# Eight small slope diagonals in the opening of an attention kernel: six built by ScalarE ahead of its first cast, two by VectorE behind its own

## The chip, the cores and the metric

The kernel runs on one core of one Trainium2 chip. The metric is the device time in microseconds (us) of one execution. A profile covers one execution; its "span" is about 2 us shorter than the device time of the same run. Engines are named as in the profile: PE (TensorE matmul), PEld (its weight load), DVE (VectorE), ACT (ScalarE), POOL (GpSimd), SP (SyncE).

## The reference, cut to what matters

```python
# attention: 4 batches, 8 heads, 768 positions, head size 64; local window of 96 plus 8 global keys
scores = q @ k.T / 8
bias = -slopes[:, None, None] * dist        # one slope per head
a = softmax(where(keep, scores + bias, -1e9))
x = a @ v
# then a two-layer block over 3072 tokens of 512 (2048 hidden): relu(x @ w_in) squared, scaled and shifted, @ w_out
```

For the first two granules (256 query positions each) the kernel adds the bias by matmul: a diagonal matrix with the head's slope on it, times a common distance matrix, summed in PSUM (the tiles `ps_s` in the profile, which the matmuls write) under the scores. These eight 128x128 diagonals are what the change moves.

## The kernel before

The emission order is each engine's instruction order (ScalarE's timeline below shows its diagonals, cast, diagonals and copy in this order). These are the opening's parts; cuts are marked.

```python
    # POOL: loads of later blocks (each keeps GpSimd busy for 0.8 to 1.0 us in this trace)
    load_qk(1, 0)
    load_v(0)
    load_qk(1, 1)
    load_w_in(0, 8)
    ...
    def diagonal(hs):
        for h in hs:
            nc.scalar.activation(diag[:, h, :], ident_bf[:], ACT.Copy, scale=slopes[h] / QSCALE)

    diagonal(range(0, 4))
    ...
    cp = nc.vector.tensor_copy
    acp = nc.scalar.copy
    ...
    warm(9, 4 * P)            # nine 128x512 matmuls on zeros
    cast_first(0, 0, cp)      # VectorE: first keys, f32 to bf16
    cast_first(0, 1, acp)     # ScalarE: first queries
    diagonal(range(4, H))     # ScalarE: heads 4 to 7
    qk_first(0, 0, cp)        # TensorE transposes keys; VectorE copies them out of PSUM
    qk_first(0, 1, acp)       # TensorE transposes queries; ScalarE copies them out
    open_bias((0, 1))         # TensorE: diagonals of heads 0 to 3 times the distances
    cast_first(1, 0, cp)
    cast_first(1, 1, acp)
    for part in range(2):
        for i in (0, 1):
            u[i][1](part)     # TensorE: first score matmuls
    run(u[0][2])
    warm(4)
    ...
    open_scores((2,))
    make_koff(1, [0])
    qk_block(1, 0, (cp, cp))
    open_bias((3,))
    open_scores((3,))
    stage_A(0)                # first use of the value loads
    ...
    stage_A(2)
    qk_block(1, 1, (cp, acp)) # transposes of key and query block 1: last load of the opening
```

The softmax here doesn't subtract the row's maximum and nothing guards it: scores larger than these inputs give would overflow.

Of the kernel before, what the change touches and what calls it, by code (L numbers as in the profile page):

```python
# [17 lines left out]
def kernel(  # L18
# [13 lines left out]
    nc = tc.nc  # L32
    P = nc.NUM_PARTITIONS

    B, H, S, D = q.shape
# [17 lines left out]
    QSCALE = 1.0 / float(D) ** 0.5  # L53
# [130 lines left out]
    ident_bf = const.tile([P, P], BF16, name="ident_bf")  # L184
# [42 lines left out]
    slopes = [float(2.0 ** (-8.0 * (h + 1) / H)) for h in range(H)]  # L227
    diag = open_bf[:, 3 : 3 + H, :]

    def diagonal(hs):  # L230
        for h in hs:
            nc.scalar.activation(diag[:, h, :], ident_bf[:], ACT.Copy, scale=slopes[h] / QSCALE)  # L232

    diagonal(range(0, 4))

    tmpl = const.tile([P, H, 6, P], BF16, name="tmpl")

# [20 lines left out]
    def cast_first(h2, n, copy):  # L258
        hs = slice(h2 * H // 2, (h2 + 1) * H // 2)
        copy(  # L260
            nat[0][:, n, :, hs, :],
            first_f32[h2, n][:].rearrange("p h (s d) -> p s h d", s=GB),
        )
# [57 lines left out]
    def qk_first(h2, n, evac):  # L321

        ps = ps_h.tile([P, GB, 2, P], BF16, name="ps_t", tag="psh")
        for i in range(GB):
            for c in range(2):
                hp = 2 * h2 + c
                nc.tensor.transpose(
                    ps[:, i, c, :], nat[0][:, n, i, 2 * hp : 2 * hp + 2, :], ident_bf[:]
                )
        dst = qk_of(0, n)[:, 0:GB, 2 * h2 : 2 * h2 + 2, :]  # L330
        evac(  # L331
            dst.rearrange("p b c (m s) -> p c b m s", s=GB),
            ps[:].rearrange("p s c (b m) -> p c b m s", b=GB),
        )
# [675 lines left out]
    warm(9, 4 * P)  # L1010
    cast_first(0, 0, cp)
    cast_first(0, 1, acp)
    diagonal(range(4, H))
    qk_first(0, 0, cp)
    qk_first(0, 1, acp)
    open_bias((0, 1))
# [234 lines left out]
```

## Time and profile before

The time is 208.95 us (median of three runs, 208.86 to 208.96). The profiled run has a span of 206.6 us; at 208.37 us it was faster than any of the three.

| reading | value | view |
|---|---|---|
| TensorE busy | 201.7 of 206.6 us | page, part 1 |
| TensorE's share of the chain that ended last | 95% | page, part 4 |
| four diagonals between cast and copy | 0.90 us on ScalarE | timeline |
| last query transpose ends | 5.92 + 0.22 = 6.14 us | timeline, single matmul |
| query copy starts | 6.24 us | timeline |
| first score matmuls | 6.86 us | chain |

The page of before: engine, busy us, share, instruction count; then shares of the chain of waits by engine.

```profile
PE 201.7 (98%) x2191; PEld 160.2 (78%) x2191; DVE 159.7 (77%) x336; ACT 128.6 (62%) x200; POOL 70.1 (34%) x90
...
PE 95%; DMA 2%; ACT 1%; DVE 0%; issue 0%
```

The chain of waits of before, cut to the first 10 us. Columns: start, us, what.

```profile
0.74 4.14 DMA first<-in_q_dram
...
4.91 0.62 ACT nat L260
5.53 0.81 ACT open_bf L232 x4
6.33 0.48 ACT qx L331
...
6.86 0.51 PE ps_s L441 x12
```

The chain puts 0.81 us on the four diagonals (`open_bf` L232) because they are the last thing ahead of the copy in ScalarE's order. What they cost is only how much longer they last than the copy's other condition, the query transposes. The timeline of ScalarE of before (columns: start, us, engine, line, operation, out<-in, count, idle time before and what ended it):

```profile
3.17 0.91 ACT L232 ACTIVATE open_bf<-ident_bf 128x128 bf16<-128x128 bf16 x4
4.91 0.62 ACT L260 CAST nat<-first 128x512 bf16<-128x512 f32 x1 [0.83 <-DMA first<-in_q_dram]
5.43 0.90 ACT L232 ACTIVATE open_bf<-ident_bf 128x128 bf16<-128x128 bf16 x4
6.24 0.56 ACT L331 COPY qx<-ps_t 128x512 bf16<-128x512 bf16 x1
6.89 0.62 ACT L260 CAST nat<-first 128x512 bf16<-128x512 f32 x1
```

ScalarE idles for 0.83 us ahead of the cast, room for more diagonals. And the eight first transposes of before (durations in ns: minimum, median, maximum):

```profile
L327 PE MATMUL ps_t<-ident_bf,nat x8: 219/288/314, 5.3 to 5.9; 128*128 128x128 bf16 x8
```

VectorE of before, where three operations took longer than their size asks (later in the same trace a 128x512 cast takes 0.44 us, and a 128x128 bf16 copy 0.20):

```profile
2.72 0.64 DVE L192 CAST open_bf<-rel 128x256 bf16<-128x256 f32 x1
...
3.62 0.50 DVE L194 TENSOR_SCALAR open_bf<-open_bf 8x128 bf16<-8x128 bf16 x1
...
4.44 0.79 DVE L260 CAST nat<-first 128x512 bf16<-128x512 f32 x1 [0.32 <-DMA first<-in_k_dram]
```

### The profile page before, as it was taken

How to read it: one execution, taken by the hardware profiler on the slowest of the kernel's cores; microseconds unless marked ns; L12 is line 12 of the kernel's file. 1: busy time of each engine (PE TensorE's matmuls, PEld its weight loads, DVE VectorE, ACT ScalarE, POOL GpSimd, SP SyncE). 2: the span in 40 equal slices, each digit the busy share in tenths (PEclk: the TensorE clock that was granted, in tenths of full speed). 3: DMA queues.
4: the chain of work that ended last, by engine and by line, in shares of the span. 5: the costliest groups of instructions: out<-in, count | busy, mean ns of one | idle time of the engine just before them, and what ended most of it. 6: DMA issues, size and time to landing. Idle time of an engine off the chain costs nothing.

```text
span 206.6 us, 5323 instructions
## 1 busy us (share of the span) xinstructions
PE 201.7 (98%) x2191; PEld 160.2 (78%) x2191; DVE 159.7 (77%) x336; ACT 128.6 (62%) x200; POOL 70.1 (34%) x90
## 2 busy tenths in 40 slices
PE   7999999999999999999999999999999999999993
PEld 2678884557867585878888898888888889888883
DVE  7586589977989866799799975699866696737974
ACT  4975669486976558685664595663695764476200
POOL 8995333899357300913700908200000000000000
PEclk9999999999999999999999999999999999999999
DMA  6999999999999999999999999993460300240006
GB/s 166 172 179 201 207 207 177 155 153 134 126 146 118 155 140 209 206 193 212 139 217 160 118 155 195 189 189 57 53 206 3 98 9 0 61 145 0 0 9 197
DMA packets 110836, 28.17 MB, mean 136 GB/s; under 512 B 97852, under 2 KB 109308, under 8 KB 110812
## 3 DMA queue, kind: packets, MB, share of 16 engines
q0 software_dynamic: 76000, 13.11, 87.6%
q1 hardware_dynamic: 33612, 14.13, 39.5%
q10 hardware_dynamic: 1200, 0.59, 1.1%
q8 instruction: 17, 0.28, 0.6%
q14 instruction: 7, 0.06, 0.1%
HBM read 27.26 MB, written 6.29 MB: 162 GB/s over the span
## 4 chain that ended last, share of the span: by engine, by line
PE 95%; DMA 2%; ACT 1%; DVE 0%; issue 0%
PE ps L619 41%; PE ps L819 24%; PE ps L667 14%; PE ps_s L441 6%; PE ps_av L495 5%; DMA first<-in_q_dram 2%; PE ps_t L351 1%; PE ps_s L517 1%; PE ps_x L591 1%; PE ps_s L532 1%; PE ps_av L558 1%; ACT qx L331 1%; PE ps_t L341 0%; PE ps_last L819 0%; ACT open_bf L232 0%; ACT nat L260 0%
## 5 line engine op out<-in xcount | busy, mean ns | idle before, releaser
L619 PE MATMUL ps<-xT,w_in_bf 128*128 128x256 bf16 x768 | 90.3, 273 | 0.0
L629 ACT ACTIVATE gT<-ps 128x512 bf16<-128x512 f32 x96 | 55.8, 598 | 46.8 <-PE ps L619 46.6
L619 PEld LDWEIGHTS <-w_in_bf 128*128 128x128 bf16 x768 | 73.0, 98 | 9.4 <-DVE xT L594 0.2
L450 ACT ACTIVATE pt<-ps_s 128x1024 bf16<-128x1024 f32 (+1 forms) x44 | 39.3, 946 | 2.7 <-PE ps_s L441 2.7
L667 PE MATMUL ps<-w_out_bf,gT 128*128 128x512 bf16 x128 | 29.7, 380 | 0.0
L457 DVE TENSOR_TENSOR pt<-pt,tmpl 128x1024 bf16<-128x1024 bf16 (+1 forms) x40 | 24.5, 645 | 3.8 <-ACT pt L450 3.7
L819 PEld LDWEIGHTS <-gsum 128*128 128x128 bf16 x256 | 24.1, 98 | 3.7 <-DVE gsum L782 0.5
L108 POOL DMA_DIRECT2D vb<-in_v_dram x24 | 21.6, 915 | 6.3 <-DMA w_out_bf<-in_moe_w_out_dram 3.3
L793 DVE TENSOR_TENSOR gT<-gT 128x1024 bf16<-128x1024 bf16 x20 | 13.7, 686 | 11.7 <-ACT gT L629 11.7
L667 PEld LDWEIGHTS <-gT 128*128 128x128 bf16 x128 | 11.8, 98 | 13.0
L466 DVE TENSOR_TENSOR xn<-ps_av,rc 128x256 bf16<-128x256 f32 x48 | 20.4, 424 | 1.7
L819 PEld LDWEIGHTS <-gT 128*128 128x128 bf16 x200 | 18.6, 98 | 2.3
L465 DVE RECIPROCAL rc<-ps_av 128x4 f32<-128x4 f32 x48 | 8.6, 179 | 12.3 <-PE ps_av L495 10.4
L495 PEld LDWEIGHTS <-pt 128*128 128x128 bf16 x320 | 14.4, 98 | 2.7 <-DVE xn L466 0.7
L116 POOL DMA_DIRECT2D nat<-in_k_dram x16 | 14.4, 897 | 5.5 <-DMA w_in_bf<-in_moe_w_in_dram 2.4
L116 POOL DMA_DIRECT2D nat<-in_q_dram x16 | 14.2, 888 | 4.9 <-DMA nat<-in_q_dram 3.1
L632 DVE TENSOR_TENSOR gT<-gT 128x512 bf16<-128x512 bf16 x32 | 12.9, 421 | 3.6 <-ACT gT L629 3.3
L495 PE MATMUL ps_av<-vb,pt 128*128 128x65 bf16 x208 | 15.4, 193 | 0.0
L819 PE MATMUL ps<-w_out_bf,gsum 128*128 128x256 bf16 x128 | 15.3, 273 | 0.0
L819 PE MATMUL ps<-wsub,gsum 128*128 128x256 bf16 x128 | 15.1, 273 | 0.0
L122 POOL COPY gate<-xT 1x1 bf16<-1x1 bf16 x6 | 1.9, 313 | 36.7 <-DMA xT<-xn 36.7
L819 PE MATMUL ps<-w_out_bf,gT 128*128 128x256 bf16 x120 | 13.9, 273 | 0.0
(111 smaller groups left out, 226.6 us busy)
## 6 DMA issues: line engine op xcount, KB each, us to landing
out_dram<-o_q SPq DMA_DIRECT2D x15, 256.0 KB, 2.4
vb<-in_v_dram POOLq DMA_DIRECT2D x24, 128.0 KB, 7.4
nat<-in_k_dram POOLq DMA_DIRECT2D x22, 128.0 KB, 7.0
nat<-in_q_dram POOLq DMA_DIRECT2D x22, 128.0 KB, 6.7
w_out_bf<-in_moe_w_out_dram POOLq DMA_DIRECT2D x4, 512.0 KB, 16.1
w_in_bf<-in_moe_w_in_dram POOLq DMA_DIRECT2D x4, 256.0 KB, 7.4
w_in_bf<-in_moe_w_in_dram POOLq DMA_DIRECT2D x2, 512.0 KB, 11.2
out_dram<-o_sb SPq DMA_DIRECT2D x4, 256.0 KB, 6.3
```

What stands on the lines that cost most here:

```text
L108: nc.gpsimd.dma_start(vbuf[b % 2][:, sb, :, 0:D], rows_of(v, b, sb))
L116: nc.gpsimd.dma_start(t[:, n, i, :, :], rows_of(srcs[n], b, sb))
L450: nc.scalar.activation(pt[:, :, 0:ncol], ps[:, :, 0:ncol], ACT.Exp, scale=QSCALE)
L457: nc.vector.tensor_tensor(pv, pv, m.rearrange("p h a c -> p h (a c)"), ALU.mult)
L466: nc.vector.tensor_tensor(dst, av[:, :, :, 0:D], rc[:].to_broadcast((P, 2, 2, D)), ALU.mult)
L495: nc.tensor.matmul(av[:, i, hi, 0 : D + 1], lhsT=pt[:, hi, c * P : (c + 1) * P], rhs=vv, start=(n == 0), stop=(n == len(terms) - 1),)
L619: nc.tensor.matmul(ps[:, i, :], lhsT=w_in_bf[:, kc, fc * P : (fc + 1) * P], rhs=xT[j][:, kc, :], start=(kc == 0), stop=(kc == KC - 1),)
L629: nc.scalar.activation(gs, ps[:], ACT.Relu)
L632: nc.vector.tensor_tensor(gs, gs, gs, ALU.mult)
L667: nc.tensor.matmul(po[:], lhsT=g_of(j)[:, fc, tb * P : (tb + 1) * P], rhs=w_out_bf[:, fc, :], start=(fc == 0), stop=(fc == FC - 1),)
L793: outs.append(lambda: nc.vector.tensor_tensor(gs, gs, gs, ALU.mult))
L819: nc.tensor.matmul(ps[:, tb, cs], lhsT=stat[:, fc, tb * P : (tb + 1) * P], rhs=mov[:, fc, cs], start=(fc == 0), stop=(fc == NH - 1),)
```

## The change

Its intent is to leave nothing between ScalarE's cast and its copy of the queries, by using idle time of ScalarE (before the cast) and of VectorE (between its cast and its copy).

```diff
-    diagonal(range(0, 4))
+    diagonal(range(0, 6))
@@
     cast_first(0, 0, cp)
     cast_first(0, 1, acp)
-    diagonal(range(4, H))
+    for h in range(6, H):
+        nc.vector.tensor_scalar_mul(diag[:, h, :], ident_bf[:], slopes[h] / QSCALE)
     qk_first(0, 0, cp)
```

The instruction order of each engine is otherwise the same; TensorE's is the same matmul for matmul, so one can subtract the start of the n-th matmul in one trace from that in another.

## The prediction

> **What bounds the kernel now.** The chain of waits that ended last is 95% TensorE; TensorE is busy 201.7 of 206.6 us at clock 1.0, and by the table of stretches idles only 1.2 us at the start, 0.07 us between 5.28 and 6.90 us, 0.28 us between 8.4 and 10 us, a little at the end. VectorE and ScalarE count only where they hold TensorE up. In the chain, cut to the first 10 us, the lines that the change touches are: load of q (to 4.89), ScalarE cast (4.91), four diagonals (5.53 to 6.33), query copy (6.33 to 6.81), then the first score matmuls (6.86). The intent is to take those four diagonals off that chain.
>
> **Costs.** A diagonal on ScalarE lasts 293 ns and starts 0.20 us after the one before (timeline). [...] Two more ahead of the first cast end near 4.5 us; ScalarE waits for q until 4.91 anyway: free. On VectorE the two multiplies take about 0.18 us each (estimate from the 128x128 bf16 copy, 0.20 us). They start near 5.2 us, behind the key cast, and VectorE idles until the key copy at 5.93: also free, if not held up.
>
> **What is saved.** Not 0.8 us. The query copy needs the query transposes, which TensorE ends at 6.14 (timeline of single matmuls); the copy starts at 6.24 today. So at most about 0.08 us of the four diagonals is exposed. Behind it, TensorE works on bias matmuls until 6.79 and the key copy's weight load comes at 6.72, so the score matmuls can move from 6.86 to about 6.80: 0.06 us. The second q load lands near 6.85 (issue plus 5.6 us), so the second cast, at 6.89, will not move; TensorE does not wait for it, since warm-up matmuls run to 7.91. From there TensorE runs nearly gap-free, so 0.06 us should reach the end.
>
> **What may eat it.** [...] three VectorE ops that began 0.35 to 0.40 us into a load's descriptor writing took 0.64, 0.50 and 0.79 us (the last a cast that took 0.44 us later). The new multiplies begin about 0.28 us into one. If both are blocked the key copy slips by up to 0.1 us; if they block GpSimd, the next query load (lands 11.92, used near 12.06) slips and TensorE may lose up to 0.15 us. I expect one multiply to slip in and the other to wait till about 5.7 us: no harm.
>
> **Prediction.** 208.95 - 0.05 = 208.90 us, between 208.6 and 209.15 (8 in 10). Faster by over 2%: 0.005; within 2%: 0.99; slower by over 2%: 0.005.
>
> **What would show it.** Right: ScalarE has six diagonals from 3.17, none between cast and copy; query copy starts near 6.16; score matmuls near 6.80; second cast still at 6.89; key copy still at 5.93. Wrong: the key copy starts after 6.0 or the score matmuls not before 6.86 (no gain), the transposes at 11.86 show a wait for a load (loss), or a gain over 0.2 us, which would mean that something later hung on this and my reading of the nearly gap-free TensorE was too simple.
>
> **What would make it wrong.** A shift of GpSimd's loads that meets TensorE later, or drift between sessions; both are as large as the gain itself.

Two passages are cut where marked: a formula for ScalarE beside the measured 293 ns, and what was said of GpSimd and VectorE before the three operations. The sum is 208.95 - 0.05 = 208.90 us, the 0.05 standing for the gain that "What is saved" puts at 0.06. "What may eat it" rests on the three operations alone. Its "descriptor writing" is what the trace shows as DMA_DIRECT2D on GpSimd, 0.8 to 1.0 us a load and without a break from 1.34 to 13.1 us; the three operations began 0.37, 0.40 and 0.35 us into one. That they were blocked by it was the author's estimate.

## The result, and the profile after

The changed kernel took 208.70 us (median of four runs, 208.63 to 209.15); the kernel before, with the run added in that session, 208.91 us (208.52 to 208.96). The ratio is 0.9999 with a 95% interval of 0.998 to 1.0017. Ratios here are the mean time of one kernel's runs over the mean of the other's in the same rounds, so not quite the ratio of the medians.

The profiled run happened to be the slowest of the four (209.15 us, span 207.4). Its page:

```profile
PE 202.1 (97%) x2191; PEld 160.1 (77%) x2191; DVE 161.3 (78%) x338; ACT 128.5 (62%) x198; POOL 68.9 (33%) x90
...
PE 65%; DMA 23%; POOL 9%; issue 1%; DVE 0%; POOLq 0%
```

TensorE is as busy as before. Its share of the chain fell because this chain runs back from a late wait at 69 us (below) through loads and GpSimd.

ScalarE after:

```profile
3.17 1.31 ACT L232 ACTIVATE open_bf<-ident_bf 128x128 bf16<-128x128 bf16 x6
4.94 0.62 ACT L260 CAST nat<-first 128x512 bf16<-128x512 f32 x1 [0.46 <-DMA first<-in_q_dram]
6.05 0.58 ACT L331 COPY qx<-ps_t 128x512 bf16<-128x512 bf16 x1 [0.49 <-PE ps_t L327]
6.88 0.62 ACT L260 CAST nat<-first 128x512 bf16<-128x512 f32 x1 [0.25 <-DMA first<-in_q_dram]
```

The copy now waits for the transposes, as intended, and starts 0.20 us sooner. But the transposes end sooner too: 6.01 instead of 6.14. They are faster, each of them, though the change touches none:

```profile
L327 PE MATMUL ps_t<-ident_bf,nat x8: 219/219/230, 5.3 to 5.8; 128*128 128x128 bf16 x8
```

The first score matmuls after (6.86 before):

```profile
6.68 0.51 PE L441 MATMUL ps_s<-qx,kx 64*128 64x128 bf16 x12
```

VectorE after:

```profile
4.49 0.75 DVE L260 CAST nat<-first 128x512 bf16<-128x512 f32 x1 [0.36 <-DMA first<-in_k_dram]
5.16 0.72 DVE L1014 TENSOR_SCALAR open_bf<-ident_bf 128x128 bf16<-128x128 bf16 x2
5.73 0.69 DVE L331 COPY kx<-ps_t 128x512 bf16<-128x512 bf16 x1
```

The two multiplies end at 5.88, one after 0.18 us and the other after 0.63; the key copy starts 0.04 us after the last key transpose, as before.

Now the subtraction, matmul for matmul, after minus before (start times from the trace's records):

| at (us in before) | matmul | after minus before |
|---|---|---|
| 6.86 | first scores | -0.17 |
| 10.53 | third matmul of the first `stage_A`, the first that reads value block 1 | -0.12 |
| 12.11 | fifth transpose of key and query block 1, the first that reads the query load | -0.07 |
| to 59.1 | all | -0.06 |
| 68.4 | third score matmul of a later block | +0.73 |
| end | last matmul | +0.74 |

So 0.17 us were won in the opening, 0.10 given back by 12.1 us, and in this run 0.8 lost at 59 and 68 us. The large one is a wait for a transposing DMA, seen in the timeline of TensorE after:

```profile
68.36 0.23 PE L441 MATMUL ps_s<-qx,kx 64*128 64x128 bf16 x2
69.10 0.34 PE L441 MATMUL ps_s<-qx,kx 64*128 64x128 bf16 x6 [0.51 <-DMA qx<-nat]
```

The other three timed runs of the changed kernel took 208.63 to 208.72 us, so this 0.8 us is no fixed cost. The questions are: why was the opening's gain 0.17 us and not the predicted 0.06, what clips it, and is the late wait the change's doing?

### The profile page after: what moved, and what is told of

The parts are those of the page before. It is cut to its first block, busy times and chain, and to the rows that moved or that the text cites. A ratio compares the mean times of both kernels' runs of the same rounds, so it can differ in the third digit from the quotient of the medians.

```text
span 207.4 us, 5323 instructions
## 1 busy us (share of the span) xinstructions
PE 202.1 (97%) x2191; PEld 160.1 (77%) x2191; DVE 161.3 (78%) x338; ACT 128.5 (62%) x198; POOL 68.9 (33%) x90
## 4 chain that ended last, share of the span: by engine, by line
PE 65%; DMA 23%; POOL 9%; issue 1%; DVE 0%; POOLq 0%
PE ps L619 29%; PE ps L819 24%; DMA nat<-in_q_dram 12%; DMA w_in_bf<-in_moe_w_in_dram 6%; PE ps L667 5%; DMA qx<-nat 4%; PE ps_s L441 4%; PE ps_av L495 3%; POOL vb L108 3%; POOL nat L102 3%; POOL w_in_bf L140 2%; POOL nat L116 1%; PE ps_last L819 0%; DVE o_last L828 0%; POOL rel L173 0%
## 5 line engine op out<-in xcount | busy, mean ns | idle before, releaser
L465 DVE RECIPROCAL rc<-ps_av 128x4 f32<-128x4 f32 x48 | 8.6, 179 | 12.3 <-PE ps_av L495 10.4
L122 POOL COPY gate<-xT 1x1 bf16<-1x1 bf16 x6 | 1.1, 176 | 35.9 <-DMA xT<-xn 35.9
## 6 DMA issues: line engine op xcount, KB each, us to landing
w_in_bf<-in_moe_w_in_dram POOLq DMA_DIRECT2D x2, 512.0 KB, 11.3
```

## The experiments

Two theories of the faster transposes. A: TensorE starts at half speed, and the moment at which it gets full speed differs from run to run, whatever the kernel. B: the change did it, for example by keeping ScalarE off the identity matrix that the transposes read. No run had shown either yet; both rest on one difference between two profiles, transposes 0.107 us apart in before and 0.056 in after.

### The kernel before again, and the changed kernel again

No edit in either.

> The kernel before, unchanged. Theory A (clock phase): the 0.107 us spacing of the first transposes in the profile of before (half speed until 5.79 us) against 0.056 us in that of after is not the change: [...] the first score matmuls start anywhere from 6.68 to 7.3 us. Theory B (the change moved them): the transposes are at half speed until 5.8 us again, score matmuls at 6.86. Time 208.9, spread of single runs 0.4 us, ratio 1.000.

> The changed kernel, unchanged. Theory A: the clock switch moves here too; the query copy starts 0.04 us after the last query transpose whatever the clock does (before: 0.10 us). Theory B: full speed from 5.29 again, score matmuls at 6.68. The stall of 0.5 us at 68 us for the transposed queries, seen once in the profile of after, comes and goes with the loads: single runs from 208.5 to 209.2. Ratio to before 0.9995 to 1.000.

What is cut from the first is a range for the moment of the switch that no run had shown; the measured moments follow.

Measured: before again 208.62 us (208.43 to 208.92), ratio 0.9994 (0.9982 to 1.0006); after again 208.61 (208.39 to 209.63), ratio 0.9997 (0.9981 to 1.0013), both against 208.86 (208.56 to 209.1). The single runs of after again spread wider than the expected 208.5 to 209.2. The unchanged kernel, second profile: the transposes, ScalarE and the first scores:

```profile
L327 PE MATMUL ps_t<-ident_bf,nat x8: 289/314/314, 5.3 to 6.0; 128*128 128x128 bf16 x8
...
5.36 0.90 ACT L232 ACTIVATE open_bf<-ident_bf 128x128 bf16<-128x128 bf16 x4
6.38 0.59 ACT L331 COPY qx<-ps_t 128x512 bf16<-128x512 bf16 x1
...
7.33 0.28 PE L441 MATMUL ps_s<-qx,kx 64*128 64x128 bf16 x4
```

Here all eight transposes ran at half speed: most took 314 ns, 0.107 us apart, where after has 219 ns and 0.056 us (the clock records of before and after hold two values, 1.0 and 0.5), and full speed comes only after them. The times of these clock records are in the packed traces and no `prof` view prints them. They have the switch to full speed at 5.82 us in the first profile of before, 7.04 in before again, 5.14 in after and 4.97 in after again; the warm-up matmuls began at 1.19 in all four. Over the ten runs told here whose first matmul came at 1.19 us with at least nine warm-ups the switch came between 3.95 and 7.04 us, so 2.8 to 5.8 us after that matmul. In all the traces told here, every stretch at full speed lasted a whole number of times 3.413 us (2, 58, 59 or 61; 201.39 us, 59 times, in before and in after). Two runs further on rule out B: the kernel before (loads late) was at full speed from 5.48, the changed kernel (loads late) at half until 6.24. So A stands.

Two things follow. First, the unchanged kernel's first scores came at 7.33 us here against 6.86 in its first profile, +0.47, and its last matmul came 0.48 us later too: a delay of the opening goes to the end undiminished, and the clock's moment alone moves this kernel by more than the whole expected gain. (At half speed the first scores do not even wait for the copy, which ended at 6.96: the bias matmuls of `open_bias` kept TensorE busy until then.) Second, the diagonals ended at 6.26, before the last transpose (6.03 + 0.31 = 6.34). The copy waited for the transposes alone: in this run there was nothing for the change to save.

After again had full speed, 219 ns per transpose, but its first query load came late (cast at 5.15), and the first scores started at 6.89. Measured from the cast's end (5.77) they took 1.13 us, as in the first profile of after.

### Four more diagonals in the way; the VectorE half left out

```diff
 # on the kernel before
     diagonal(range(4, H))
+    diagonal(range(4, H))
```

> Kernel before, its four diagonals between cast and copy done twice (eight in all). ScalarE then ends them near 7.13 us and the query copy starts near 7.05 instead of 6.24. Theory 1 (the opening is on the chain and TensorE is gap-free after it): the first score matmuls come near 7.67 us and the run takes 0.8 us longer, 209.7. Rival (waits for loads further on take up what the opening loses): under 0.3 us longer.

```diff
 # on the changed kernel
-    for h in range(6, H):
-        nc.vector.tensor_scalar_mul(diag[:, h, :], ident_bf[:], slopes[h] / QSCALE)
+    diagonal(range(6, H))
```

> Changed kernel, but the last two diagonals stay on ScalarE between cast and copy, none on VectorE. They should end near 5.95 us, before the query transposes (6.01 to 6.14), so the copy starts as in the changed kernel, 0.04 us after the last transpose: same time. If instead the VectorE half matters, the copy is late by up to 0.1 us, or the VectorE ops after the key cast (the cast at 6.33, the koff copies at 8.7 and 9.3, which the changed kernel's profile shows longer than before's) get back to 0.44, 0.34 and 0.18 us.

Measured: four more diagonals gave 209.64 us (209.43 to 210.26), ratio 1.005 (1.0035 to 1.0064), which on 208.86 is +1.0 us with 0.7 to 1.3 as the interval. Its ScalarE:

```profile
5.05 0.62 ACT L260 CAST nat<-first 128x512 bf16<-128x512 f32 x1 [0.97 <-DMA first<-in_q_dram]
5.58 1.70 ACT L232 ACTIVATE open_bf<-ident_bf 128x128 bf16<-128x128 bf16 x8
7.18 0.56 ACT L331 COPY qx<-ps_t 128x512 bf16<-128x512 bf16 x1
```

The copy started 1.51 us after the cast's end (5.67), where 0.72 + 0.80 was expected. Against before, the first scores came 0.94 us later and the last matmul 1.04. The opening is on the chain and its losses are paid in full; theory 1 stands.

Without the VectorE half: 208.58 us (208.5 to 208.89), ratio 0.9992 (0.9979 to 1.0005).

```profile
5.04 0.62 ACT L260 CAST nat<-first 128x512 bf16<-128x512 f32 x1 [0.56 <-DMA first<-in_q_dram]
5.57 0.50 ACT L232 ACTIVATE open_bf<-ident_bf 128x128 bf16<-128x128 bf16 x2
6.36 0.59 ACT L331 COPY qx<-ps_t 128x512 bf16<-128x512 bf16 x1 [0.28 <-PE ps_t L327]
```

With two diagonals left between cast and copy, ScalarE still idled for 0.28 us before the copy. This run was at half speed up to 6.18 us. At full speed the two would end 0.41 us after the cast (6.07 - 5.66) and the transposes 0.45 us after it (6.01 - 5.56 in after), so even then they should not be in the way; that is an estimate from these two traces. So the VectorE half was needed neither at this run's clock, nor, by the estimate, at full speed. Of the VectorE times that the expectation names, the second key cast was back at 0.44 us, but the two koff copies (`make_koff`) took 0.29 and 0.64; in before again they took 0.77 and 0.60, so they vary without the change.

### Forcing the clock

To compare both kernels at full speed, the first loads were issued late, behind idle activations, with longer warm-up.

```diff
 # on either kernel
+    pause = const.tile([P, 2 * P], F32, name="pause")
+    ... nine activations pause<-pause on ScalarE, then all four first loads issued by ScalarE
-    warm(9, 4 * P)
+    warm(24, 4 * P)
```

> Kernel before with the first loads issued by ScalarE alone after nine idle activations, and 24 warm-up matmuls: TensorE must then be at full speed when the first q comes, and GpSimd's loads land long before they are used. Theory (the four diagonals are exposed by what they last beyond the query transposes, and that depends on the clock): the query copy starts about 0.72 us after the cast's end, 0.26 us after the last query transpose. Total about 212.

> The changed kernel with the same late loads. Theory: the query copy starts 0.04 us after the last query transpose, about 0.22 us sooner after the cast than in the run above; the first score matmuls come about 0.2 us sooner after the cast, and the total is 0.2 us (0.1%) less than above. Rival (the change is worth 0.06 us at most, whatever the clock): both copies within 0.1 us of each other.

Both missed the state that they were made for: 219.17 us (218.01 to 219.5) and 218.03 (217.57 to 218.39), where 212 was expected. Issued from 5.62 us on, the first keys came near 11.6 and 11.3 us, about 6 us after issue (in before they landed 3.7 us after it), the first queries near 13.1 and 12.1; I take it that they stood in line with GpSimd's loads. TensorE idled for 2.79 and 2.65 us before its first transposes. In the first run the query transposes were at half speed and the copy started 0.05 us after them; in the second they were still at full speed and it started 0.04 us after them. (From the cast's end it was 0.72 and 0.49 us, as expected.) The two were not in the same state, and their difference in time is not used.

The opposite, half speed in both:

```diff
 # on either kernel
-    warm(9, 4 * P)
+    warm(2, 4 * P)
```

> Kernel before with two warm-up matmuls in place of nine. Theory (clock): TensorE is at half speed through the whole opening, the query transposes end near 6.35, later than the diagonals, the copy starts 0.04 us after them, and the first score matmuls come at 7.3 or later; the run is 0.5 to 1.5 us longer than before. Rival (the clock plays no part): the copy starts at 6.24 as in the first profile of before and the time is the same.

> The changed kernel with two warm-up matmuls in place of nine. Theory: no diagonal is exposed in either, so query copy and first score matmuls stand as far behind the q cast as in the run above, within 0.05 us, and the times agree within their spread. Rival (the diagonals cost 0.06 us or more whatever the clock): copy and score matmuls come sooner after the cast than above.

Measured: 210.34 us (209.51 to 210.54), ratio 1.0071, and 210.50 (209.91 to 210.57), ratio 1.0088. Full speed now came at 8.55 and 9.37 us by the clock records. Seven warm-up matmuls fewer cost 1.5 to 1.8 us (0.0071 and 0.0088 of 208.64), more than anything the change touches. The intervals of the two ratios overlap (1.005 to 1.0092 and 1.0072 to 1.0103). Before at half speed:

```profile
5.37 0.90 ACT L232 ACTIVATE open_bf<-ident_bf 128x128 bf16<-128x128 bf16 x4
6.37 0.59 ACT L331 COPY qx<-ps_t 128x512 bf16<-128x512 bf16 x1
```

After at half speed:

```profile
6.40 0.58 ACT L331 COPY qx<-ps_t 128x512 bf16<-128x512 bf16 x1 [0.70 <-PE ps_t L327]
```

The copies start 0.04 us after the last query transpose in both (6.34 and 6.36), the first scores at 7.55 and 7.58. The expectation had put them the same distance behind the cast; that was wrong, since the cast ended 0.24 us apart (5.46 and 5.70) and the slow transposes, not the cast, set the time. The point holds: at half speed the change saves nothing.

Then full speed again, with the first query cast alone held back:

```diff
 # on either kernel, behind the diagonals ahead of the cast
+    ...                       # the tile pause, cleared by VectorE
+    for _ in range(13):
+        nc.scalar.activation(pause[:], pause[:], ACT.Copy, scale=1.0)
-    warm(9, 4 * P)
+    warm(26, 4 * P)
```

> Repair of the two warm_late runs, which missed: their loads came so late that TensorE fell back to half speed. Here the loads stay as they are; 13 idle activations hold only the first q cast back to about 9.8 us, and 26 warm-up matmuls bridge the wait, so TensorE is at full speed at the query transposes. Kernel before otherwise. Theory: the query copy starts 0.72 us after the cast's end and about 0.26 us after the last query transpose. Total about 214.2.

> The changed kernel with the same two additions. Theory: the copy starts 0.49 us after the cast's end, 0.04 us after the last query transpose, so 0.22 us sooner than above; the loads land long before they are used, so the 0.2 us reach the end: ratio to the run above 0.999. Rival (the change is worth at most 0.06 us at any clock, or is lost later): copies within 0.1 us, last matmuls within 0.1 us.

Measured: before 213.38 us (213.37 to 213.39, four runs); after 214.29 (213.29 to 214.9, six runs in three clumps: 213.3, 213.8, 214.8). Before, all transposes at full speed:

```profile
10.61 0.40 PE L332 MATMUL ps_t<-ident_bf,nat 128*128 128x128 bf16 x4 [1.52 <-ACT nat L265]
...
10.46 0.90 ACT L232 ACTIVATE open_bf<-ident_bf 128x128 bf16<-128x128 bf16 x4
11.27 0.56 ACT L336 COPY qx<-ps_t 128x512 bf16<-128x512 bf16 x1
```

The last query transpose ended at 11.00 and the copy started 0.26 us after it: as expected. A copy that waits for nothing else starts 0.04 us after it, so 0.22 us of the diagonals is exposed at full speed. The run of after missed its state. Its profile got full speed early, at 3.95 us, so it ended the warm-up early, idled longer, and fell back to half speed:

```profile
8.16 0.39 PE L332 MATMUL ps_t<-ident_bf,nat 128*128 128x128 bf16 x4
10.72 0.59 PE L332 MATMUL ps_t<-ident_bf,nat 128*128 128x128 bf16 x4 [2.17 <-ACT nat L265]
```

Four equal transposes took 0.39 us before an idle time of 2.17 us and 0.59 after it. The clock record has the fall at 10.78, at the end of a stretch of 3.41 us in which TensorE had been busy for 1.24. In before with the cast held back, four transposes still took 0.40 us after 1.52 us without a matmul, in a stretch of 3.41 us with 1.67 us busy. The totals of this pair therefore compare two clock states and not the change. The record lists the mean granted clock of every run: 0.990 in the three runs of after at 214.8 to 214.9, 0.998 to 1.0 in the other three and in all runs of before. So the upper clump is such a state; 213.8 against 213.3 stays unexplained. The two runs of after at 213.3 (213.29 and 213.31) lie 0.06 to 0.10 us below all four of before; picked afterwards as they are, they are a hint of a gain and no more.

### The loads that clip the gain

In the table above the gain shrinks at the first matmul that reads value block 1 and at the first transpose that reads query block 1. The value load was issued by GpSimd at 4.09 and landed 6.3 us later, at about 10.4 (DMA view of after); the matmul before it started at 10.33, it itself at 10.42, 0.09 us apart where before shows 0.04. In after again the same gap was 0.14 us, with that load landing near 10.6. The query load was issued at 5.81 and landed near 12.0; the transpose started at 12.04. Each of the three waiting matmuls began 0.04 to 0.05 us after the landing. My theory was that GpSimd's issuing sets these times.

```diff
 # on either kernel
     load_v(0)
+    late_f = const.tile([P, 2 * P], F32, name="late_f")
+    for _ in range(3):
+        nc.gpsimd.iota(late_f[:], ...)     # idle work, about 1 us
     load_qk(1, 1)
```

> Kernel before with three idle iotas (about 1 us) on GpSimd ahead of the loads of key and query block 1, whose query load landed near 12.0. Theory (that load caps what the opening can gain): the fifth of the block's eight transposes starts near 13.0 whatever the clock and the opening did before; all later work is 0.5 to 0.9 us later than usual, total 209.5. Rival (the load has slack): the total does not change.

> The changed kernel with the same three iotas. Theory: the fifth transpose starts at the same time as in the run above within 0.05 us, although the first score matmuls may start up to 0.5 us apart; so the change is worth nothing here and the totals agree. Rival: the difference at the first score matmuls is still there behind the transposes.

Measured: 208.73 us (208.53 to 208.86), ratio 1.0002 (0.9985 to 1.0018), and 208.78 (208.36 to 209.1), ratio 1.0001 (0.9984 to 1.0018). The rival of the first run won: no change. The rival of the second won too: the first scores of the two runs stood 0.13 us apart (6.88 and 7.01), and so did the fifth transposes (12.14 and 12.27), which both came after the landing and did not wait. GpSimd in before:

```profile
4.95 0.90 POOL L102 DMA_DIRECT2D nat<-in_k_dram  x1
5.82 0.91 POOL L102 DMA_DIRECT2D nat<-in_q_dram  x1
```

GpSimd with the iotas, on the kernel before:

```profile
4.97 1.34 POOL L201 IOTA late_f<- 128x256 f32 x3
6.26 1.05 POOL L102 DMA_DIRECT2D nat<-in_k_dram  x1
7.30 0.88 POOL L102 DMA_DIRECT2D nat<-in_q_dram  x1
```

The query load was issued 1.48 us later (7.30 against 5.82) and the DMA view has it landing after 4.6 us instead of 6.1: at 11.94 and 11.96. In that stretch the DMA view (6 to 12 us, both runs) shows the engines busy for 90% or more of every slice, so I take it that they set the landing and that GpSimd only lengthens or shortens the line. So the clip is real (the waits of 0.05 to 0.1 us in the two profiles of after), but when GpSimd issues the query load is not its cause. The value load was issued ahead of the iotas, so its landing was not tested, and no run here moved either.

One of these runs gave by luck what the forced pairs had missed. The kernel before with iotas got full speed at 5.48 us and its query cast at 4.93, within 0.01 us of the first profile of after:

```profile
L333 PE MATMUL ps_t<-ident_bf,nat x8: 219/220/286, 5.3 to 5.8; 128*128 128x128 bf16 x8
...
4.93 0.62 ACT L266 CAST nat<-first 128x512 bf16<-128x512 f32 x1 [0.85 <-DMA first<-in_q_dram]
5.45 0.90 ACT L238 ACTIVATE open_bf<-ident_bf 128x128 bf16<-128x128 bf16 x4
6.26 0.56 ACT L337 COPY qx<-ps_t 128x512 bf16<-128x512 bf16 x1
```

Transposes end at 6.00 (after: 6.01), copy at 6.26 (after: 6.05), first scores at 6.88 (after: 6.68). At full speed the change wins 0.20 us at the first scores: 0.22 of exposed diagonals less 0.02 for a copy of 0.58 instead of 0.56 us. Counted from the end of the query cast, the first scores came after 1.33 us in this run, in before and in before with the cast held back, and after 1.13 in both profiles of after that were at full speed.

The openings side by side (us; clock by the clock records; the third column, less the 0.04 that even a copy that waits for nothing else needs, is what the diagonals cost). Left out: four more diagonals (0.92, scores 7.80) and the three runs that missed their state.

| run | clock at the transposes | copy minus end of last query transpose | first scores |
|---|---|---|---|
| before | half, full from 5.82 | 0.10 | 6.86 |
| before again | half (full from 7.04) | 0.04 | 7.33 |
| before, two warm-ups | half (full from 8.55) | 0.04 | 7.55 |
| before, loads late | half, full from 5.48 | 0.26 | 6.88 |
| before, cast held back | full (from 5.05) | 0.26 | 11.88 |
| after | full (from 5.14) | 0.04 | 6.68 |
| after again | full (from 4.97) | 0.04 | 6.89 |
| after, loads late | half, full from 6.24 | 0.04 | 7.01 |
| after, two warm-ups | half (full from 9.37) | 0.04 | 7.58 |
| after, diagonals on ScalarE alone | half, full from 6.18 | 0.04 | 7.00 |

## Why the prediction was right or wrong

**The time was right**, and so was "within 2%": 208.70 us lies in 208.6 to 209.15. But the predicted gain of 0.05 us is a fifteenth of the interval of the ratio (0.998 to 1.0017 is 0.77 us wide), so the time could not have told it from nothing, or from 0.2: a forecast of no gain would have been as right. What can be judged is each step, by the start of the same instruction in the traces.

**"Not 0.8 us": right.** The chain charged 0.81 us to the diagonals, and what they cost is what they outlast the transposes by.

**"At most about 0.08 us of the four diagonals is exposed": the step that was mis-sized.** For the trace that it was read from it is right: the copy's lag went from 0.10 to 0.04, so 0.06. But it was a reading of one clock state, half speed until 5.82 us. At half speed the exposure is 0 (0.01 in before with late first loads), at full speed 0.22 (0.26 - 0.04). The transposes' durations in that very profile, 219 to 314 ns, would have said so.

**"Score matmuls near 6.80": wrong, 6.68.** The prediction held two ends fixed that move with the clock: that of the query transposes (6.14; 6.01 in after) and that of the bias matmuls (6.79; 6.66 in after). By where it shows, the -0.17 is -0.13 (transposes' end), -0.06 (the copy's lag) and +0.02 (the longer copy). But these are not shares of clock and change: in before the copy waits for its diagonals, 0.72 us after the cast's end whether the clock switches at 5.05, 5.48 or 5.82, so the faster clock alone would have won it nothing. At the clock of after the change is worth 0.20, and a cast that ended 0.03 later took 0.03 back. The key copy at 5.73 instead of the expected 5.93 is the clock alone.

**"The second cast will not move": right**, 6.88 against 6.89.

**"One multiply slips in and the other waits till about 5.7": right in kind.** The first took 0.18 us, though it began 0.21 us into GpSimd's 0.91 us on a load; the second ended at 5.88; neither held up the key copy. The traces show VectorE operations whose end goes with GpSimd's work on a load. The first key cast shows it best: in four runs it began at 4.37, 4.49, 4.59 and 4.70, took 0.88, 0.75, 0.65 and 0.55 us, and ended at 5.24 or 5.25 each time. So the arrival of its own load did not matter; a wait for GpSimd's work on a load (from 4.09 to 4.98) fits. The second multiply of after ended 0.02 us after GpSimd's work on a load (5.88 and 5.86), in after again too (5.89 and 5.87), and with iotas in that load's place it ended at 5.58. How the one holds up the other the traces do not show.

**"If they block GpSimd, the next query load slips": the danger did not exist.** GpSimd issued that load at 5.81 (before: 5.82), and in the run with iotas a load issued 1.48 us later landed at the same time.

**"TensorE runs nearly gap-free, so it should reach the end": right for losses, not for gains.** +0.47 stayed +0.48, and four more diagonals cost +1.0. But a gain of 0.17 shrank to 0.07 at two loads that landed at 10.4 and 12.0 us.

**What stays open.** First, the wait at 59 to 68 us. Subtracting from each trace that of before, the six profiles of kernels with the multiplies on VectorE move by 0.81, 0.18, 0.56, 0.21, 0.04 and 0.01 us between 20 us and the end (after, after again, loads late, first loads late, cast held back, two warm-ups). The seven without them move by 0.01 or less, but for one with 0.07; diagonals on ScalarE alone is among them. That points to a small effect of the multiplies through the loads, but it can be chance: the whole times show no difference (ratios 0.9999 and 0.9997), and no run here was made to tell. Second, the end-to-end worth of the change at full speed was never measured, because both forced pairs fell out of their state.

No version clearly better than both kernels came out. Six diagonals ahead and two between, all on ScalarE, is the simpler form and took the same time.

## What to carry to other kernels

The chain of waits charges a group with all its time, even when something else would have released the next step a moment later; before moving it, find that other condition, subtract, and ask whether it moves with the clock. Before reading a difference of 0.2 us as the change's, profile the unchanged kernel twice and subtract the starts of the same instruction: here that alone gave 0.47 us. In this kernel the opening passed losses on whole (+0.47 us as +0.48), but of a gain of 0.17 only 0.07 got past the loads that landed at 10.4 and 12.0 us.
